# Spreading a load burst, stretching a norm with its shift as a channel bias, and moving operand splits between phases and engines

## The chip, the cores and the metric

The kernel runs on one core of a Trainium2 chip. The metric is the device time of one execution in microseconds (us). The engines are TensorE (PE, with its weight loads listed as PEld), VectorE (DVE), ScalarE (ACT), GpSimd (POOL) and SyncE (SP). Each has its own list of instructions, and they wait for one another through semaphores. In this kernel SP issues every DMA, one after the other.

## The reference

One transformer block on `x[1, 2048, 576]` in float32, with an adaptive layer norm whose shifts, scales and gates come from a conditioning vector `c`.

```python
mod = (silu(c) @ w_mod)                       # six rows of 576: sa, ca, ga, sb, cb, gb
h = layernorm(x) * (1 + ca) + sa
q = (h @ wq), 32 heads of 128                 # k, v from caches of 16 heads, the last 512 positions
o = softmax(q k^T / sqrt(128)) v
x = x + ga * (o @ wo)                         # wo: 4096 x 576
h = layernorm(x) * (1 + cb) + sb              # the second norm
x = x + gb * ((sigmoid(h @ w_gate) * (h @ w_up)) @ w_down)     # F = 4608
```

## The kernel before

Every product is made of three matmuls: an operand is split into a high part in the fp32r format (ACT copies it) and the low rest (a subtraction on DVE or POOL), and hi x hi, hi x lo and lo x hi are added in PSUM. The three large products of the second half are computed by a seven-product scheme on 2 x 2 blocks (as Strassen's), so that sums of weight blocks and of activation blocks are needed besides the blocks themselves. The 2048 rows of `x` are four blocks of 512 (`xs[0]` to `xs[3]`), and a block has four tiles `t` of 128 rows.

The program has three phases.

*Attention*, 0 to about 1420 us. A loop over N = 512 steps, one for each pair of a head and a block, with query projection, scores (`st`, `qt`, `kt`), softmax (`pp`, `ptt`), and the product with v (`ot`). The softmax sums `rs` go out to memory (`rscr<-rs`) and come back as a broadcast (`rb<-rscr`), by which DVE scales the output (`ov`); `oscr<-ov` stores it. Work in the background of the steps is written with `at_n(n, ...)`, which runs a function at step n. A planner lays out a list `jobs` of weight preparations that use parts of `xs` as rooms: `ab` and `tail` jobs make the sums of gate and up weights, split the tail rows and store them in `wsc`; `wo` jobs scale the output weights by the first gate, sum and split them and store them in `wosc`; `down` jobs scale the down weights and store their sums, unsplit, in `dsc`. Every `tail` job ends with small stores `wsc<-x` (24 in all, in four parts). The modulation rows for scale, shift and gates are fetched every 32 steps (`wm`, `wmt`).

*Projection*, about 1420 to 1844 us. VISITS = 32 visits `v`, each of seven stages of 12 matmuls (128x288), of which every stage adds its PSUM result to `x` on DVE. The values come from `vr<-oscr`, are summed on POOL (`vt`, four operations a visit) and split on ACT and DVE (`vh`); the weights come from `wosc` into slots `wb` and `wc`. `late_step` runs in the last steps of attention and issues the first loads of this phase; `beside(v, s)` runs after each stage, and in the last eight visits it takes the statistics of blocks 0 and 1 (`ln_stats`, `ln_ready`), normalizes their tiles (`early_norm(t)`) and makes the sums of the seven-product scheme (`early_sums(t)`), which are put in the scratch tensor `scr[0]`. `park_x` stores the residual rows. `stage_first` reads `scr[0]` back into the tiles `ts` and the rooms in `xs`; `load_combo` transposes a combination by PE (`w<-ident`), and ACT and DVE split it from PSUM into `hc`.

*FFN*, about 1844 us to the end. U = 72 units (36 for each pair of blocks), each of seven products of 7 matmuls (128x512, `a`, `b`, `c`), with the matmuls of the down product of earlier units (`w<-sd,hl`, three of 128x288 at a time) between them. After each product `split_w` splits the next gate/up operand (ACT `sw<-sr`, DVE `sw<-sr,sw`; five buffers) and `load_w` loads a later one (`sr<-wsc`, four buffers). After each four down groups `split_sd` splits a down operand (ACT, POOL `sd<-dr,sd`) and `load_sd` loads one (`dr<-dsc`, three buffers). The gating products (`g`, `v`) are on DVE and ACT, their sums `vs` and splits `hl` on POOL and ACT. At u = 4, 9, 14 and 19 `late_tile` does the second norm of a tile of blocks 2 and 3 and puts its sums in `scr[1]`.

What sets the order: an engine's instructions stand in program order, and `pin` keeps single instructions at the place where they are written against the scheduler, so the hand-written positions decide what stands ahead of what on each queue.

## Time and profile before

| | us |
|---|---|
| median of 3 runs | 3145.04 (3144.78 to 3145.11) |
| the profiled execution | 3147.1 |
| span in its profile | 3145.3 |
| mean granted TensorE clock of the span | 0.986 |
| PE busy | 3048.5 (97%) |
| DVE, ACT, POOL busy | 2288.3, 1721.0, 1655.2 |

The profile is of one execution. PE's busy time is near the span, so the idle time of PE and the stretches in which its granted clock is below 1 are what can be read as lost. A row of the timeline has the start, the duration, the engine, the line of the source (here always that of a helper, so the names of the tiles tell the rows apart), output and inputs, and in brackets the idle time of the engine just before it and what ended that.

### The profile page before, as it was taken

What the parts mean: (1) busy time and instruction counts of PE and PEld (TensorE: products, weight loads), DVE (VectorE), ACT (ScalarE), POOL (GpSimd) and SP (SyncE); (2) the same over time, 40 slices, a digit from 0 to 9 for tenths busy, and PEclk for the clock granted to TensorE, in tenths of its full rate; (3) what the DMA queues carried; (4) which work ended last, traced back from release to release, by engine and by line L of the source; (5) the groups of instructions that cost most, each with busy time, mean ns of one, the idle gap of its engine ahead of it and who ended that gap; (6) DMA issues with size and microseconds to landing.
All of it is one profiled execution on the core that took longest, in us unless ns stands there. A gap on an engine that the chain in (4) does not pass through costs nothing.

```text
span 3145.3 us, 49956 instructions
## 1 busy us (share of the span) xinstructions
PE 3048.5 (97%) x16629; PEld 2619.5 (83%) x16629; DVE 2288.3 (73%) x4116; ACT 1721.0 (55%) x3569; POOL 1655.2 (53%) x1531
## 2 busy tenths in 40 slices
PE   8999999999999999998999889999999989999998
PEld 6888788878888888887999777888888878888887
DVE  6666666687666666666888868777777877777778
ACT  5666555656666655553333344555555645555553
POOL 2344333335666555303555626766665665665664
PEclk9999999999999999999999899999999999999999
DMA  4677877775777766547545254434434443343342
GB/s 118 182 197 213 216 189 191 178 197 137 216 225 219 217 197 195 154 126 269 185 170 185 104 201 144 130 108 131 143 111 115 135 149 112 107 117 111 111 123 79
DMA packets 435570, 503.86 MB, mean 160 GB/s; under 512 B 51184, under 2 KB 392816, under 8 KB 426096
## 3 DMA queue, kind: packets, MB, share of 16 engines
q1 hardware_dynamic: 434704, 500.67, 54.3%
q8 instruction: 131, 2.15, 0.3%
q14 instruction: 127, 1.04, 0.1%
q10 hardware_dynamic: 608, 0.00, 0.0%
HBM read 347.72 MB, written 152.81 MB: 159 GB/s over the span
## 4 chain that ended last, share of the span: by engine, by line
PE 87%; DVE 5%; POOL 3%; DMA 3%; issue 2%; ACT 1%; SPq 1%; ACTq 0%; DVEq 0%; POOLq 0%
PE a L36 19%; PE st L36 18%; PE qp L36 13%; PE w L36 12%; PE ot L36 11%; PE c L36 10%; PE b L36 5%; DVE x L36 2%; POOL x L36 1%; DMA rscr<-rs 1%; DMA sr<-wsc 1%; SPq L36 1%; DVE sw L36 1%; POOL h L36 0%; DVE v L36 0%
## 5 line engine op out<-in xcount | busy, mean ns | idle before, releaser
L36 PEld LDWEIGHTS w<-sd,hl 128*128 128x128 f32 x3036 | 516.5, 189 | 109.7 <-DVE x L36 18.6
L36 PE MATMUL a<-hc,sw 128*128 128x512 f32 x2016 | 588.5, 396 | 15.9 <-DVE v L36 13.9
L36 PE MATMUL w<-sd,hl 128*128 128x288 f32 x3036 | 574.5, 299 | 15.5 <-DVE x L36 14.5
L36 DVE TENSOR_TENSOR x<-w,x 128x288 f32<-128x288 f32 x980 | 429.3, 452 | 197.2 <-PE w L36 192.2
L36 DVE TENSOR_REDUCE neg<-st 128x1 f32<-128x512 f32 x512 | 352.4, 688 | 280.1 <-PE st L36 279.9
L36 ACT ACTIVATE ptt<-st 128x512 fp32r<-128x512 f32 x512 | 306.1, 598 | 433.9 <-PE st L36 433.4
L36 PE MATMUL ot<-ptt,vs 128*128 128x512 f32 x1536 | 486.1, 425 | 1.7 <-DVE ptt L36 1.7
L36 PE MATMUL st<-kt,qt 128*128 128x512 f32 x1536 | 447.0, 398 | 4.0 <-ACT pp L36 4.0
L36 PE MATMUL qp<-hTm,wa 128*128 128x512 f32 x1536 | 446.9, 400 | 3.9 <-DVE qt L36 2.1
L36 DVE TENSOR_TENSOR ptt<-st,ptt 128x512 fp32r<-128x512 f32 x512 | 351.9, 688 | 133.4 <-ACT ptt L36 132.6
L36 PEld LDWEIGHTS a<-hc,sw 128*128 128x128 f32 x2016 | 356.3, 189 | 56.9 <-DVE v L36 17.6
L36 ACT ACTIVATE pp<-st,neg 128x512 f32<-128x512 f32 x512 | 350.3, 684 | 48.2 <-DVE neg L36 47.7
L36 DVE TENSOR_TENSOR sw<-sr,sw 128x256 fp32r<-128x256 f32 x504 | 289.8, 576 | 101.9 <-ACT sw L36 75.1
L36 PEld LDWEIGHTS st<-kt,qt 128*128 128x128 f32 x1536 | 289.2, 189 | 71.6 <-ACT pp L36 5.6
L36 PEld LDWEIGHTS qp<-hTm,wa 128*128 128x128 f32 x1536 | 286.3, 189 | 72.0 <-DVE qt L36 5.5
L36 ACT ACTIVATE sw<-sr 128x384 fp32r<-128x384 f32 x504 | 259.0, 515 | 153.6 <-issue 83.3
L36 POOL TENSOR_TENSOR x<-x 128x256 f32<-128x256 f32 (+3 forms) x334 | 246.7, 758 | 153.6 <-DMA x<-in_B_w_up_dram 101.1
L36 PEld LDWEIGHTS st<-ident,pp 128*128 128x128 f32 x2048 | 255.6, 141 | 77.4 <-issue 4.3
L36 PE MATMUL st<-ident,pp 128*128 128x128 f32 x2048 | 308.8, 274 | 5.3 <-DVE rs L36 2.8
L36 POOL TENSOR_TENSOR sd<-dr,sd 128x288 fp32r<-128x288 f32 x249 | 217.2, 874 | 181.3 <-ACT sd L36 181.3
L36 PE MATMUL c<-hc,sw 128*128 128x512 f32 x1008 | 304.5, 395 | 0.0
L36 PEld LDWEIGHTS ot<-ptt,vs 128*128 128x128 f32 x1536 | 253.6, 191 | 28.1 <-DVE ptt L36 3.1
(168 smaller groups left out, 4747.1 us busy)
## 6 DMA issues: line engine op xcount, KB each, us to landing
sr<-wsc SPq DMA_DIRECT2D x504, 192.0 KB
dr<-dsc SPq DMA_DIRECT2D x249, 144.0 KB
rb<-rscr SPq DMA_DIRECT2D x128, 256.0 KB
oscr<-ov SPq DMA_DIRECT2D x64, 512.0 KB
vr<-oscr SPq DMA_DIRECT2D x32, 1024.0 KB
wsc<-x SPq DMA_DIRECT2D x36, 896.0 KB
wosc<-x SPq DMA_DIRECT2D x32, 1008.0 KB
dsc<-x SPq DMA_DIRECT2D x17, 1008.0 KB
```

What stands on the lines that cost most here:

```text
L36: i = got(*args, **kw)
```

## The change

1. `late_step` issues the five loads `w_load(0, s)` at k = 1, 3, 5, 8 and 11 of the last steps and the second `v_load` at k = 13, where all stood at k = 0. The loop that allocated PSUM tags `w`, `b` and `c` at the start of the projection, with no work in it, is gone; the tags get their banks in the order of use.
2. The second norm of blocks 0 and 1. The shift row is not added to the tiles any more. `shift_cols` (at step 110 of attention) turns the row into columns `fcol` by six PE transposes of one row, and `load_combo` applies it as a bias for each channel: ACT Identity with bias, and one DVE operation with two inputs and a scalar. The scale is multiplied on POOL for block 0 and on DVE for block 1. The steps for a tile stand five stages apart (norm, scale, two puts, sums, four puts), `park_x` goes tile by tile, and the first `stage_first` and `load_combo` stand at other stages.
3. `late_tile` loses its two POOL additions of the shift.
4. The planner has two lists, `jobs` (ab, tail) and `wide` (wo, down), with a due time for each. `down` jobs split their sums (ACT and POOL) and store both parts; `dsc` is twice as large, and in `dsc` and `wosc` the high and low parts are axis 1.
5. In the FFN `load_sd` loads the split operand (`sd<-dsc`, 288 KB, seven buffers); `split_sd` and `dr` are gone. The low part of `split_w` is made on POOL and DVE in turn.
6. The calls between projection and FFN stand in another order.

The core of the diff, without the parts on layout:

```diff
         if k == 0:
             v_load(0)
-            for s in range(5):
-                w_load(0, s)
+        if k in (1, 3, 5, 8, 11):
+            w_load(0, (1, 3, 5, 8, 11).index(k))
+        if k == 13:
             v_load(1)
...
-    for tag, bufs in (("w", 4), ("b", 1), ("c", 1)):
-        for _ in range(bufs):
-            fpsum(tag, bufs, [P, BLK])
...
     def early_norm(t):
+        for b in range(2):
+            h = xs[b][:, t, :]
+            nc.scalar.activation(h, h, AF.Identity, scale=LN[b][1][:, t : t + 1], bias=NMR[b][:, t : t + 1])
+
+    def early_scale(t):
         for b, eng in ((0, nc.gpsimd), (1, nc.vector)):
             h = xs[b][:, t, :]
-            mv, y = LN[b][:2]
-            nc.scalar.activation(h, h, AF.Identity, scale=y[:, t : t + 1], bias=NMR[b][:, t : t + 1])
-            nc.gpsimd.tensor_mul(h, h, rows2["scale"])
-            eng.tensor_add(h, h, rows2["shift"])
+            eng.tensor_mul(h, h, rows2["scale"])
...
-            nc.scalar.activation(hc[:, s, :], p, AF.Copy)
-            if s < 2:
-                nc.vector.tensor_sub(hc[:, 3 + s, :], p, f32(hc[:, s, :]))
+            kind = {B11: 0, T3: 2}.get(c, 1)
+            if c in (T1, T4):
+                nc.scalar.activation(hc[:, s, :], p, AF.Copy)
             else:
-                r = slice(P // 2, P)
-                nc.vector.tensor_sub(hc[r, 2, :], p[r], f32(hc[r, 2, :]))
+                nc.scalar.activation(hc[:, s, :], p, AF.Identity, bias=fcol[:, kind, s : s + 1])
+            r, to = (slice(0, P), 3 + s) if s < 2 else (slice(P // 2, P), 2)
+            if c in (T1, T4):
+                nc.vector.tensor_sub(hc[r, to, :], p[r], f32(hc[r, s, :]))
+            else:
+                nc.vector.scalar_tensor_tensor(hc[r, to, :], p[r], fcol[r, kind, s : s + 1], f32(hc[r, s, :]),
+                                               op0=OP.add, op1=OP.subtract)
...
+    def shift_cols():
+        row = rows2["shift"]
+        p = ps_wo()
+        for half in range(2):
+            e = wp.tile([P, 4, TQ], F32, tag="hd", name="hd", bufs=1)
+            n0 = half * D2
+            pin(nc.gpsimd.tensor_copy(e, row[:, None, n0 + 2 * P : n0 + D2].to_broadcast([P, 4, TQ])))
+            for k in range(3):
+                src = row[0:1, n0 + k * P : n0 + (k + 1) * P] if k < 2 else e.rearrange("p q d -> p (q d)")[0:1]
+                pin(nc.tensor.transpose(p[:, 3 * half + k : 3 * half + k + 1], src, ident[0:1, 0:1]))
...
+    at_n(110, shift_cols)
...
-        nc.vector.tensor_sub(t[:, 3:5], r[:, 0:2], f32(t[:, 0:2]))
+        turn[0] += 1
+        (nc.gpsimd if turn[0] % 2 else nc.vector).tensor_sub(t[:, 3:5], r[:, 0:2], f32(t[:, 0:2]))
...
-            t = fpool["p"].tile([P, D2], F32, tag="dr", name="dr", bufs=3)
-            d = nc.sync.dma_start(t, dsc[g % NG][:, a if g == GL else WITH[a]])
+            t = fpool["p"].tile([P, 2, D2], F32R, tag="sd", name="sd", bufs=7)
+            d = nc.sync.dma_start(f32(t), dsc[g % NG][:, :, a if g == GL else WITH[a]])
...
-            nc.gpsimd.tensor_add(h, h, rows2["shift"])
...
     for _ in range(4):
         load_w(True)
+    for k in range(4, 10):
+        stage_first(k)
     for _ in range(4):
         split_w()
-        load_w(True)
-    for k in range(4, 10):
-        stage_first(k)
     load_combo(0, 1, True)
     for k in range(10, 14):
         stage_first(k)
-    for _ in range(3):
-        load_sd(True)
-    for _ in range(5):
-        split_sd()
+    for _ in range(4):
+        load_w(True)
+    for _ in range(7):
         load_sd(True)
```

How the rows of the queues move, at three places. On SP, where attention ends and the projection's first loads are issued, before:

```order
L36 DMA vr<-oscr_0_286 128x2048
L36 DMA wb_15152<-wosc_354 128x2304
L36 DMA wb_15154<-wosc_354 128x2304
L36 DMA wb_15156<-wosc_354 128x2304
L36 DMA wb_15158<-wosc_354 128x2304
L36 DMA wb_15160<-wosc_354 128x2304
L36 DMA vr<-oscr_0_286 128x2048
L36 DMA rscr_284<-rs 128x4
L36 DMA rb<-rscr_284 128x512
L36 DMA rscr_285<-rs 128x4
L36 DMA rb<-rscr_285 128x512
L36 DMA oscr_3_293<-ov 512x1x256 x2
```

and now:

```order
L36 DMA vr<-oscr_0_286 128x2048
L36 DMA rscr_284<-rs 128x4
L36 DMA wb_15276<-wosc_354 128x8x288
L36 DMA rb<-rscr_284 128x512
L36 DMA wb_15318<-wosc_354 128x8x288
L36 DMA rscr_285<-rs 128x4
L36 DMA wb_15353<-wosc_354 128x8x288
L36 DMA rb<-rscr_285 128x512
L36 DMA oscr_3_293<-ov 512x1x256
L36 DMA wb_15380<-wosc_354 128x8x288
L36 DMA wb_15395<-wosc_354 128x8x288
L36 DMA oscr_3_293<-ov 512x1x256
```

The five weight loads stood ahead of the last two trips of the softmax sums; now they stand among them, the second `vr` behind all of them. Of the fetch of the last modulation row on SP, near step 114: 18 tail stores (`wsc_312`, `wsc_313`, `wsc_314`, six each) stood in the rows just ahead of it, and six stand there now.

On POOL, at the last four visits of the projection (`x_101` is block 0, `x_102` block 1, the digits behind `scale` and `shift` are buffer numbers), before:

```order
L36 TENSOR_TENSOR vt<-vr,vt 128x512
L36 TENSOR_TENSOR x_101<-x_101,scale_2152 128x576
L36 TENSOR_TENSOR x_101<-x_101,shift_3131 128x576
L36 TENSOR_TENSOR x_101<-x_101,scale_2152 128x576
L36 TENSOR_TENSOR x_101<-x_101,shift_3131 128x576
L36 TENSOR_TENSOR x_101<-x_101,scale_2152 128x576
L36 TENSOR_TENSOR x_101<-x_101,shift_3131 128x576
L36 TENSOR_TENSOR vt<-vr 128x512
L36 TENSOR_TENSOR x_101<-x_101,scale_2152 128x576
L36 TENSOR_TENSOR x_102<-x_102,scale_2152 128x576
L36 TENSOR_TENSOR vr<-vr 128x4x128
L36 TENSOR_TENSOR x_101<-x_101,shift_3131 128x576
```

and now:

```order
L36 TENSOR_TENSOR vt<-vr,vt 128x512
L36 TENSOR_TENSOR x_101<-x_101,scale_2153 128x576 x3
L36 TENSOR_TENSOR vt<-vr 128x512
L36 TENSOR_TENSOR vr<-vr 128x4x128
L36 TENSOR_TENSOR x_101<-x_102,x_101 128x288
L36 TENSOR_TENSOR vt<-vt,vr 128x512
L36 TENSOR_TENSOR x_101<-x_101,scale_2153 128x576
L36 TENSOR_TENSOR x_102<-x_102,x_101 128x288
L36 TENSOR_TENSOR vt<-vr,vt 128x512
L36 TENSOR_TENSOR x_101<-x_102,x_101 128x288
L36 TENSOR_TENSOR x_102<-x_102,x_101 128x288
L36 TENSOR_TENSOR vt<-vr 128x512
```

The run of multiplications and additions is gone; three multiplications of block 0 stand together in the queue, and the sums of the scheme (`x_101<-x_102,x_101`) come among the `vt` sums. In the source those three are five stages apart; they are not pinned, so the order of the built program has them where their inputs are ready.

On SP, where the FFN's first loads are issued (`scr_294` is `scr[0]`), before:

```order
L36 DMA scr_294<-x_101 128x288
L36 DMA scr_294<-x_102 128x288 x2
L36 DMA scr_294<-x_101 128x288
L36 DMA ts<-scr_294 128x576 x4
L36 DMA sr<-wsc_300 128x384 x6
L36 DMA sr<-wsc_301 128x384
L36 DMA sr<-wsc_300 128x384
L36 DMA x_101<-scr_294 128x576 x4
L36 DMA x_102<-scr_294 128x576 x4
L36 DMA ts<-scr_294 128x576 x2
L36 DMA dr<-dsc_336 128x288 x3
```

and now:

```order
L36 DMA scr_294<-x_102 128x288
L36 DMA ts<-scr_294 128x576 x4
L36 DMA scr_294<-x_101 128x288
L36 DMA scr_294<-x_102 128x288 x2
L36 DMA scr_294<-x_101 128x288
L36 DMA sr<-wsc_300 128x384 x4
L36 DMA x_101<-scr_294 128x576 x4
L36 DMA x_102<-scr_294 128x576 x4
L36 DMA ts<-scr_294 128x576 x2
L36 DMA sr<-wsc_300 128x384 x2
L36 DMA sr<-wsc_301 128x384
```

Four `sr` loads stand ahead of the reads of `scr[0]` where eight stood, and the `ts` reads stand ahead of the last tile's puts.

More of the change, by code (lines that the diff above doesn't have):

```diff
@@ L686, in adaln_block_kernel @@
             jobs.append(("tail", f - 3))
-    jobs += [("wo", g) for g in range(H // 2)] + [("down", g) for g in range(NF // 2)]
+    wide = [("wo", g) for g in range(H // 2)] + [("down", g) for g in range(NF // 2)]
     BG = {}
@@ L761, in bg_split @@
     def bg_split(k, part):
-        if jobs[k][0] == "tail":
+        if k[0] == "tail":
             r, m, hi = BG[k]
@@ L765, in bg_split @@
         else:
-            a, b = ((0, 4), (4, 7))[part]
+            a, b = ((0, 4), (4, 8 if k == ("down", NF // 2 - 1) else 7))[part]
             v, hi = BG[k][0][:, a:b], BG[k][1]
@@ L782, in bg_store @@
                 pin(nc.sync.dma_start(wsc[f][:, :, 0:2], BG[k][:, 0:7]))
-            elif kind == "down":
-                n = 8 if f == NF // 2 - 1 else 7
-                pin(nc.sync.dma_start(dsc[f][:, :n], BG[k][0][:, :n]))
-            else:
-                for i in range(2):
-                    pin(nc.sync.dma_start(wosc[f // 4][:, :, i, f % 4], BG[k][1 - i][:, :7]))
-    free = {0: 9, 1: 9, 2: 7, 3: 7}
-    n = 9
-    for k, (kind, f) in enumerate(jobs):
-        need = 2 if kind == "wo" else 1
-        while True:
-            got = sorted((free[r], r) for r in range(NB) if free[r] <= n and
-                         n < N - 46 and not (r > 1 and n1 - 50 < n < n1 + 4))
-            if len(got) >= need:
-                break
+                return
+            n = 8 if k == ("down", NF // 2 - 1) else 7
+            for i in range(2):
+                to = wosc[f // 4][:, i, f % 4] if kind == "wo" else dsc[f][:, i, :n]
+                pin(nc.sync.dma_start(to, BG[k][1 - i][:, :n]))
+    free = {0: 9, 1: 9, 2: 7, 3: 7}
+    n, due = 9, 9.0
+    while jobs or wide:
+        assert n < N - 44, (n, len(jobs), len(wide))
+        got = [r for _, r in sorted((free[r], r) for r in range(NB) if free[r] <= n)
+               if not (r > 1 and n1 - 50 < n < n1 + 4)]
+        two = n > 130 and len(got) > 1 and wide and (not jobs or not n1 - 50 < n < n1 + 4)
+        if due > n or not got or not (two or jobs):
             n += 1
-            assert n < N
-        rooms = [r for _, r in got[:need]]
+            continue
+        k = (wide if two else jobs).pop(0)
+        kind = k[0]
+        rooms = got[: 2 if two else 1]
         for r in rooms:
-            free[r] = n + 14
+            free[r] = n + {"ab": 10, "tail": 13}.get(kind, 12)
         at_n(n, bg_load, k, rooms)
```

102 lines of the change are left out of this document (52 added, 50 removed).

## The prediction

> **What bounds the kernel now.** I read the head of the page first: the engine shares.
>
> ```profile
> span 3145.3 us, 49956 instructions
> PE 3048.5 (97%) x16629; PEld 2619.5 (83%) x16629; DVE 2288.3 (73%) x4116; ACT 1721.0 (55%) x3569; POOL 1655.2 (53%) x1531
> ```
>
> TensorE is busy for 97% of the span. The change removes almost no matmul work, so it can only win time in which PE idles or runs at a low granted clock. The second view is therefore a table by stage (window; busy us and instructions of PE, PEld, DVE, ACT, POOL; granted clock; DMA share; GB/s).
>
> ```profile
> ...
> 360.00:380.00 20.00, 16.40 (x72) 13.16 (x71) 9.73 (x16) 11.93 (x28) 9.12 (x12) 0.83 0.90 247
> ...
> 750.00:1300.00 550.00, 550.00 (x2827) 451.66 (x2826) 373.12 (x580) 353.59 (x754) 339.24 (x301) 1.00 0.70 208
> 1430.00:1460.00 30.00, 16.43 (x96) 14.62 (x95) 11.36 (x18) 5.78 (x12) 5.28 (x5) 0.77 0.77 269
> 1500.00:1750.00 250.00, 250.00 (x1877) 250.00 (x1876) 216.83 (x325) 98.91 (x156) 141.00 (x91) 1.00 0.47 174
> 1770.00:1850.00 80.00, 57.02 (x343) 53.55 (x343) 57.36 (x101) 26.48 (x44) 40.43 (x34) 0.83 0.34 114
> 1850.00:1960.00 110.00, 97.61 (x487) 81.52 (x488) 83.31 (x182) 57.05 (x117) 60.33 (x60) 0.95 0.57 186
> 1960.00:2240.00 280.00, 273.22 (x1449) 237.28 (x1448) 204.62 (x420) 147.98 (x304) 196.32 (x170) 0.99 0.44 130
> 2300.00:2350.00 50.00, 50.00 (x270) 43.74 (x269) 36.52 (x76) 27.22 (x56) 28.91 (x26) 1.00 0.40 113
> 2520.00:2560.00 40.00, 30.83 (x150) 25.71 (x149) 31.23 (x56) 15.88 (x34) 30.45 (x29) 0.91 0.56 176
> ...
> ```
>
> What a stage loses is its length less busy time times clock. That gives 6.4 at 360-380, 17.3 at 1430-1460, 32.7 at 1770-1850, 17.3 at 1850-1960, 9.5 at 1960-2240 and 11.9 at the pair turnover (2520-2560): 95 us, which is what the change works on. The stretches 750-1300, 1500-1750 and 2300-2350 lose nothing: PE is full at clock 1.00. The start of the kernel, the norm of blocks 2 and 3 and the kernel's last matmuls lose time too, but the change does not touch them.
>
> **The change, part by part.**
>
> *Modulation weights (360-380).* ACT waits for their fetch, and PE for ACT.
>
> ```profile
> 352.00 7.20 SPq L36 DMA_DIRECT2D wsc<-x  x10
> 361.35 0.97 SPq L36 DMA_DIRECT2D wm<-in_w_mod_dram  x2
> 366.09 1.82 ACT L36 ACTIVATE wm<-wm,cexp 128x288 f32<-128x288 f32 x4 [3.62 <-DMA wm<-in_w_mod_dram]
> 372.71 1.65 PE L36 MATMUL st<-kt,qt 128*128 128x512 f32 x3 [3.60 <-ACT pp L36]
> ```
>
> Ten tail stores take SP 7.20 us, 0.72 each. In the order of before 18 tail stores stand close ahead of this fetch; in the new order 6 do. Twelve fewer are 8.6 us, more than the 3.62 that ACT waits. Gain 5 of the 6.4, between 2 (another transfer ends last) and 6.4.
>
> *Planner and shift columns.* The down operands are now split in the attention: 18 jobs of two ACT copies and two POOL subtractions, and twice the stores. The nearest work is that of the wo jobs in 750-1300: there POOL is busy 339 of 550 us, ACT 354, DMA 0.70, and PE 550.00. With as much room left I cost it at nothing; the cover is ACT's and POOL's idle third there. Without it, the next thing late would be ACT's `pp`, as in the row at 372.71. The shift columns need six one-row PE transposes and two POOL copies (`hd`) that stand behind the weight sums. POOL waits for the loads of these sums in the row of `x<-x`:
>
> ```profile
> L36 POOL TENSOR_TENSOR x<-x 128x256 f32<-128x256 f32 (+3 forms) x334 | 246.7, 758 | 153.6 <-DMA x<-in_B_w_up_dram 101.1
> ```
>
> If PE meets one such wait it loses some us, otherwise under 1 us. I take a loss of 1, between 0 and 6.
>
> *Start of the projection (1430-1460).* SP issues two `vr` and five `wb` loads (128x2048 and 128x2304 words, 1.05 and 1.18 MB each, 8.0 MB) ahead of the last two softmax-sum round trips.
>
> ```profile
> 1417.72 4.46 SPq L36 DMA_DIRECT2D wb<-wosc  x5
> 1424.70 0.32 SPq L36 DMA_DIRECT2D rscr<-rs  x1
> 1441.81 0.32 SPq L36 DMA_DIRECT2D rb<-rscr  x1
> 1449.28 1.05 DVE L36 TENSOR_TENSOR ov<-ot,rb 128x512 f32<-128x512 f32 x1 [3.17 <-DMA rb<-rscr]
> 1450.38 3.25 PE L36 MATMUL a<-wb,vh 128*128 128x288 f32 x12 [12.85 <-DVE ov L36]
> 1459.92 1.76 PE L36 MATMUL b<-wc,vh 128*128 128x288 f32 x12
> ```
>
> The store of the sums goes out at 1424.70 and SP is let go at 1441.81, 17.1 us later; PE stands 12.85 us for the DVE `ov` that needs the result. In the new order one `wb` stands ahead of the first of these round trips and two more ahead of the second's broadcast, and the first `a` matmul waits for no DVE result any more: its PSUM bank is an attention score bank. So most of the 12.85 goes. What is late next is weights: with a load every second or third step the last `wb` and the first `wc` go out later than now. 8.0 MB between 1417.72 and 1441.81 are 332 GB/s at the least; 9.2 MB up to the first `wc` take 28 us at that rate, so 1445 if SP never waited, against 1459.92 for the first `wc` stage now. SP will wait some steps for `rs`, so I take 1451, gain 9, between 5 (those waits spread the loads further) and 13 (the whole stall goes).
>
> *End of the projection (1770-1850).* POOL runs eight multiplications and four additions of the second norm (1.55 for the one shown), among the `vt` sums; SP waits with the puts of the results, and with it the `vr` load behind them.
>
> ```profile
> 1774.44 0.15 DVE L36 TENSOR_TENSOR ln_a<-ln_y 128x4 f32<-128x4 f32 x1
> 1776.64 1.55 POOL L36 TENSOR_TENSOR x<-x,scale 128x576 f32<-128x576 f32 x1 [4.21 <-ACT x L36]
> 1776.81 1.40 DVE L36 SCALAR_TENSOR_TENSOR ln_y<-ln_a,ln_y 128x4 f32<-128x4 f32 x1
> 1779.72 25.50 SPq L36 DMA_DIRECT2D scr<-x  x6
> L36 DVE TENSOR_TENSOR vh<-vr,vh 128x512 fp32r<-128x512 f32 x109 | 109.8, 1008 | 6.4 <-ACT vh L36 4.8
> L36 DVE TENSOR_TENSOR vh<-vt,vh 128x512 fp32r<-128x512 f32 x81 | 76.4, 944 | 17.0 <-ACT vh L36 17.0
> L36 DVE TENSOR_TENSOR x<-a,x 128x288 f32<-128x288 f32 x109 | 49.1, 450 | 10.2 <-PE a L36 10.1
> L36 DVE TENSOR_TENSOR x<-x,shift 128x576 f32<-128x576 f32 x4 | 4.9, 1224 | 2.7 <-POOL x L36 2.7
> L36 DVE TENSOR_TENSOR x<-x 128x288 f32<-128x288 f32 x4 | 3.9, 986 | 4.8 <-POOL x L36 4.8
> 1841.31 1.84 PE L36 MATMUL a<-wc,vh 128*128 128x288 f32 x12
> ```
>
> (The groups `vh` and `x<-a` are of 1460-1765, the two other groups of 1770-1845; the rest are single rows.) After the change POOL has four such multiplications instead of twelve operations (three of them still together on its queue), and the puts of a tile come two to six stages behind its norm, so a `vr` load meets shorter waits ahead of it. The chain POOL-SP-`vr` dissolves, and DVE is late next. Its work from 1768 on: about 24 small norm operations at 0.37 mean between the 0.15 and 1.40 shown, 8.8; 25 `vh` at 0.99 (mean of the rows), 24.7; 26 `x` at 0.45, 11.7; four scale multiplications at 1.22, 4.9; eight half-width subtractions at 0.86 (between 0.74 alone and 0.986), 6.9. Sum 57.0, so it ends at 1825; PE's own 22 stages of 12 matmuls, at the 1877 matmuls in 250 us of its full stretch 1.6 us each, are 35 and lie beneath. The last stage ended at 1843.15 before. Gain 18. With `vh` at its undisturbed 0.68 it would be 25; if SP still holds `vr` behind puts that wait for POOL, 8.
>
> The two DVE rows, 0.15 alone and 1.40 while a POOL multiplication of 1.55 runs, are what a rule of the Trainium skill describes (SBUF — State Buffer, "SBUF: two separate sides"): VectorE with two SBUF inputs and GpSimd take the shared port pair as an exclusive lock for a whole instruction. The trace agrees for these rows. By that rule each of DVE's 25 `vh` could wait a whole POOL operation, which would add 25 x 0.3 and end this part near 1832, a gain of 11; the steady rows of 0.94 to 1.01 already hold such waits, so I leave the sum.
>
> *FFN start (1850-1960) and late tiles.*
>
> ```profile
> 1848.54 4.47 SPq L36 DMA_DIRECT2D x<-scr  x8
> 1853.56 2.20 PE L36 MATMUL w<-ident,x 128*128 128x128 f32 x8 [5.15 <-DMA x<-scr]
> 1931.20 1.62 POOL L36 TENSOR_TENSOR h<-h,shift 128x576 f32<-128x576 f32 x1
> 1932.84 4.25 SPq L36 DMA_DIRECT2D scr<-h  x2
> 1948.62 1.09 PE L36 MATMUL w<-sd,hl 128*128 128x288 f32 x3 [2.81 <-DVE x L36]
> ```
>
> PE loses 5.15 us, and some at a lower clock, to `x<-scr` loads that SP issues after eight weight loads; the new order has four ahead of them (at the 0.56 us an issue that 4.47 for eight gives, 2.2 us of SP sooner, and 0.8 MB less in flight), and the puts they read come out spread. The first late tile loses about 6 because SP stands at `scr<-h` while POOL works through multiplications, shift additions, `hl` and `sd`; two of its additions (1.6 us each) and the `sd` subtractions go. Of 17.3 lost I take 12, between 0 and 16: nothing if POOL's new `sw` work takes the place of `sd`. The three other late tiles lose 9.5 by the same chain; gain 5, between 0 and 8. The pair turnover keeps its DVE and DMA work; gain 1, between 6 and a loss of 6.
>
> *Splits in the FFN.* The steady FFN loses nothing, so nothing is won there. What moves:
>
> ```profile
> L36 POOL TENSOR_TENSOR sd<-dr,sd 128x288 fp32r<-128x288 f32 x249 | 217.2, 874 | 181.3 <-ACT sd L36 181.3
> L36 DVE TENSOR_TENSOR sw<-sr,sw 128x256 fp32r<-128x256 f32 x504 | 289.8, 576 | 101.9 <-ACT sw L36 75.1 <-PE w L36 23.5
> ```
>
> POOL gives up 217 us of `sd` and takes 252 `sw` subtractions, 191 us at the 0.758 of its 128x256 row; DVE gives up 145, ACT its `sd` copies. `sd` loads double: 249 x 144 KB more, 36 MB over 1290 us, 28 GB/s on 113 at a DMA share of 0.40. All lighter or with room; the cover is the lead of four products with which a split runs ahead (a product with its downs is some 12.75 matmuls, 2.37 us at 270 in 50 us, so 9.5 us). A queue that is in order can still make a product late, so I allow a loss of 2, between 0 and the rival's 50 below.
>
> Sum: -5 +1 -9 -18 -12 -5 -1 +2 = -47. Against the profiled execution's own 3147.1 that is 3100.1; the median of the runs is 3145.04, 2.1 less, so 3098.
>
> **Rivals.**
> 1. *DVE and the puts still bound the projection's end, and the FFN start keeps its waits.* For it: DVE is at 217 of 250 us even in steady state. Against: 25.50 us of SP waiting go with POOL's chain. Terms at 8, 5 and 4 instead of 18, 9 and 12: 3098 + 22 = 3120.
> 2. *POOL's `sw` makes products late: the slower end.* POOL's `vs` and `hl` come in runs of 1.3 to 1.5 us each and wait for ACT and DVE; a `sw` in the queue behind them can miss its product. Price: 72 units x delay. It decides from 47 / 72 = 0.65 us a unit; at 0.75 the time is 3098 + 54 = 3152. Against: the 9.5 us of lead, and POOL 29 of 50 busy. The Trainium skill warns here (GPSIMD Engine Reference, "Performance versus the Vector engine"): GpSimd takes about twice VectorE's time for two-input elementwise work. By its ratio a moved `sw` takes 1.15, 3.5 of them a unit 1.4 us more than the trace's price, and were that all exposed it would cost 100 us. The trace has 0.758 against 0.576, ratio 1.3, and measurement decides.
> 3. *More comes: late tiles and turnover stalls go as well.* Terms at 25, 13, 16, 8 and 4 give 3098 - 21 = 3077.
> 4. *The start wait is not removed, since scheduling keeps PE behind `rb`.* Then 9 is lost: 3107, inside the forecast's own range.
>
> **How the numbers follow.** The measurement of this kernel tells apart about 0.2%, 6.3 us. My forecast (3086 to 3110) has 0.50; rival 1 (to 3126) 0.25; rival 3 0.15; rival 2 0.10, of which 0.06 ends above 3151, 0.02 within 0.2% and the rest is faster. So faster 0.92, same 0.02, slower 0.06. The range 3075 to 3127 leaves out rival 2 and part of rival 3's and rival 1's ends.
>
> **What would show it.** Right: in 360-380 the 3.62 and 3.60 us waits are gone; no 12.85 before the first `a<-wb`; the last `a<-wc` ends near 20 us closer to the end of attention; POOL has no run of x multiplications and SP no 25 us at `scr<-x`; the FFN windows still read PE 50.00 with some 270 matmuls, DVE near 31 and POOL near 28 us. Wrong: fewer than 266 matmuls in 50 us of steady FFN with PE waiting for POOL `sw` or DVE; a PE wait for POOL `hd` near 345 us; a PE wait for `wc` at the projection's start as long as the old one.

## The result, and the profile after

The changed kernel takes 3107.07 us (median of 4 runs, 3105.21 to 3109.53) against 3145.07: a ratio of 0.9877 with a 95% interval of 0.986 to 0.9894, 38 us faster. The forecast was 3098 with a range of 3075 to 3127. The profiled execution took 3107.64, its span is 3105.9.

```profile
span 3105.9 us, 49158 instructions
PE 3028.0 (97%) x16635; PEld 2602.8 (84%) x16635; DVE 2184.5 (70%) x3866; ACT 1680.7 (54%) x3356; POOL 1682.8 (54%) x1556
```

The table by stage of the changed kernel, with the columns of the table of before:

```profile
360.00:380.00 20.00, 19.95 (x105) 16.32 (x104) 12.52 (x20) 15.30 (x35) 11.44 (x15) 1.00 0.79 197
660.00:700.00 40.00, 28.25 (x132) 22.46 (x131) 35.90 (x74) 14.28 (x34) 20.03 (x20) 0.87 0.60 169
1430.00:1460.00 30.00, 23.46 (x125) 19.50 (x123) 17.26 (x28) 10.28 (x23) 5.48 (x4) 0.89 0.91 292
1770.00:1850.00 80.00, 66.04 (x438) 62.48 (x437) 66.18 (x117) 34.12 (x56) 36.70 (x37) 0.94 0.56 180
1850.00:1960.00 110.00, 101.02 (x516) 84.52 (x515) 77.67 (x174) 55.98 (x108) 66.69 (x65) 0.98 0.56 177
1960.00:2240.00 280.00, 278.09 (x1500) 242.67 (x1500) 187.67 (x378) 135.56 (x255) 182.56 (x167) 1.00 0.56 166
2300.00:2350.00 50.00, 50.00 (x271) 43.73 (x271) 32.56 (x67) 23.68 (x45) 27.03 (x25) 1.00 0.53 153
```

PE is full at 360-380 now. The end of the projection (1770-1850) loses 80 - 66.04 x 0.94 = 17.9 where it lost 32.7, and the late tiles (1960-2240) 1.9 where they lost 9.5. But 660-700, where the prediction expected no change, loses 40 - 28.25 x 0.87 = 15.4. In the kernel before it lost 40 - 36.17 x 0.91 = 7.1:

```profile
660.00:700.00 40.00, 36.17 (x170) 28.59 (x169) 38.66 (x88) 18.79 (x42) 21.12 (x20) 0.91 0.65 185
```

Fixed windows shift against the work when the work moves. So I followed one DVE instruction of each step, visit or unit through both timelines and took the difference of its start times; a step of this running difference is what a place gained or lost. Its last value, -40.3, is the whole difference of the two profiled executions but for the last microsecond, so nearly all of it has a place.

```
changed kernel less kernel before, at the same instruction, us
attention (neg<-st):   step 32 +0.3 | 64 +2.7 | 112 +3.1 | 128 -0.7 | 224 -1.7 | 240 +5.5 | 288 +5.2 | 304 +7.2 | 496 +5.8 | 511 +6.5
projection (x<-b):     visit 1 +6.2 | 24 +6.2 | 27 +6.2 | 28 +3.9 | 29 -4.9 | 31 -7.6
FFN (g<-a):            unit 0 -16.2 | 2 -8.4 | 6 -14.9 | 24 -24.9 | 36 -26.5 | 40 -33.8 | 66 -38.0 | 71 -40.3
```

Between units 0 and 2 the changed kernel loses 7.8 us of its gain again, and 6.5 come back by unit 6. PE waits 4.5 us there, for ACT and POOL, where it waited 1.7 before. Every kernel of the experiments loses 5.8 us or more at this place, so none of the edits explains it, and its cause is open.

Three waits of the changed kernel answer to three of before. The chain of the modulation fetch is gone. The start of the projection and the norm of blocks 2 and 3 have waits of their own (PE rows):

```profile
688.94 1.09 PE L36 MATMUL st<-ident,pp 128*128 128x128 f32 x4 [9.77 <-DVE rs L36]
...
1449.97 2.35 PE L36 MATMUL a<-wb,vh 128*128 128x288 f32 x12 [2.50 <-DVE x L36]
1454.16 3.22 PE L36 MATMUL c<-wb,vh 128*128 128x288 f32 x12 [1.84 <-DMA wb<-wosc]
```

The row of before that answers to the first; the two others take the place of the 12.85 before the first `a<-wb`:

```profile
681.21 0.63 PE L36 MATMUL st<-ident,pp 128*128 128x128 f32 x4 [2.85 <-DVE rs L36]
```

### The profile page after: what moved, and what is told of

Its sections match the earlier page's. It is cut to its first block, busy times and chain, and to the rows that moved or that the text cites. A ratio compares the mean times of both kernels' runs of the same rounds, so it can differ in the third digit from the quotient of the medians.

```text
span 3105.9 us, 49158 instructions
## 1 busy us (share of the span) xinstructions
PE 3028.0 (97%) x16635; PEld 2602.8 (84%) x16635; DVE 2184.5 (70%) x3866; ACT 1680.7 (54%) x3356; POOL 1682.8 (54%) x1556
## 4 chain that ended last, share of the span: by engine, by line
PE 86%; DVE 5%; DMA 3%; POOL 2%; issue 1%; ACT 1%; SPq 1%; ACTq 0%; DVEq 0%; POOLq 0%
PE a L36 19%; PE st L36 17%; PE qp L36 12%; PE w L36 12%; PE ot L36 10%; PE c L36 10%; PE b L36 5%; DVE x L36 1%; SPq L36 1%; POOL x L36 1%; POOL hl L36 1%; DMA sr<-wsc 1%; DMA raw<-in_A_wq_dram 0%; POOL vs L36 0%; DVE vh L36 0%
## 5 line engine op out<-in xcount | busy, mean ns | idle before, releaser
L36 DVE TENSOR_TENSOR x<-w,x 128x288 f32<-128x288 f32 x980 | 436.4, 453 | 295.6 <-PE w L36 291.8
L36 PE MATMUL w<-sd,hl 128*128 128x288 f32 x3036 | 563.8, 295 | 6.6 <-DVE x L36 3.7
L36 POOL TENSOR_TENSOR sw<-sr,sw 128x256 fp32r<-128x256 f32 x252 | 205.3, 816 | 307.0 <-ACT sw L36 212.3
L36 PE MATMUL st<-ident,pp 128*128 128x128 f32 x2048 | 308.5, 273 | 13.8 <-DVE rs L36 10.8
L36 POOL TENSOR_TENSOR wa<-raw,wa 128x512 fp32r<-128x512 f32 (+1 forms) x128 | 112.2, 876 | 255.8 <-ACT wa L36 221.9
```

What stands on the lines that cost most here:

```text
L36: i = got(*args, **kw)
```

## The experiments

Each kernel below is the changed kernel with one edit. What is compared is the running difference to the kernel before, place by place, since single executions differ by some microseconds in places that an edit does not touch. How much can be read from the kernels whose edit lies elsewhere: their gain is -0.4 to 1.3 us over the start of the projection (last attention step to second visit), 21.9 to 24.8 from visit 24 to unit 0, 30.4 to 35.1 from visit 24 to unit 24, and 6.9 to 7.6 at the turnover (units 36 to 40). A difference inside such a span shows nothing.

**Start of the projection.** The spread, and the PSUM banks, taken back one at a time, and loads between the two.

`e1_burst`:

```diff
         if k == 0:
             v_load(0)
-        if k in (1, 3, 5, 8, 11):
-            w_load(0, (1, 3, 5, 8, 11).index(k))
-        if k == 13:
+            for s in range(5):
+                w_load(0, s)
             v_load(1)
```

> The changed kernel with its spread undone: all five w_load(0, s) and the second v_load stand at k = 0 again, while the PSUM loop stays out. Theory A (the spread only trades one wait for another: with the bank wait on ov gone, the loads should go out early): the first a stage starts near 1440 and the first b stage of the projection, which is 6.7 us later than before in the changed kernel and 6.5 us later already at the end of attention, gains 6 to 9 us; the whole 3098 to 3101. Theory B (the spread is what shortens the start, because the last rb comes sooner): PE stands for rb as before, 6 us lost against the changed kernel, 3113.

`e8_mid` has `w_load(0, k)` at k = 0 to 4 and `v_load(1)` at k = 5.

> The changed kernel with the loads between: w_load at k = 0 to 4, second v_load at k = 5. Theory A (late arrival of the weights bounds the start): the gain lies between the changed kernel and the burst or beyond the burst, 4 to 8 us, 3099 to 3103. Theory B (rb bounds): as the changed kernel, 3107, or some us worse.

`e2_banks` puts the loop `for tag, bufs in (("w", 4), ("b", 1), ("c", 1))` back.

> The changed kernel with the loop that allocates the PSUM tags w, b and c put back, so the first a matmul waits for DVE's last ov again. Theory A (start bound by the arrival of weights, the bank wait hidden beneath it): the first a starts 3 to 5 us later, but the eighth visit within 1 us of the changed kernel; 3107. Theory B (the bank wait was half of the stall): 5 us lost through to the end; 3112.

Between the last attention step and the second visit the changed kernel goes from +6.5 to +6.2 (gain 0.3), the burst from +6.0 to +8.4 (loss 2.4), the loads between from +8.4 to +7.9 (gain 0.5), and the kernel with the banks put back from +3.4 to +3.6 (loss 0.2). The whole times are 3107.4 (3106.59 to 3108.22), 3105.5 (3103.26 to 3107.32) and 3106.01 (3100.97 to 3111.71). Only the burst lies outside the scatter, so the spread is worth some 2 to 4 us, and the loads between and the banks make no difference that can be told. For the banks that is theory A. With them back, the first `a` waits for DVE's `ov` again, and by the second visit nothing of it is left:

```profile
1446.72 3.25 PE L36 MATMUL a<-wb,vh 128*128 128x288 f32 x12 [5.53 <-DVE ov L36]
```

For the loads between, the gain of 4 to 8 us of theory A did not come. Neither theory on the burst holds: the `a` matmuls start early in it, and then PE waits for DVE all the same. SP and PE of the burst:

```profile
1422.48 13.28 SPq L36 DMA_DIRECT2D wb<-wosc  x5
...
1443.61 1.75 PE L36 MATMUL a<-wb,vh 128*128 128x288 f32 x12
1445.20 1.76 PE L36 MATMUL c<-wb,vh 128*128 128x288 f32 x12
1458.29 3.25 PE L36 MATMUL a<-wb,vh 128*128 128x288 f32 x12 [11.33 <-DVE x L36]
```

PE runs two stages and stands 11.33 us at the third, whose bank is free only when DVE has added the first result to `x`; that addition stands on DVE behind the `ov` that waits for `rb`. The wait moved by two stages. And the first row shows what neither theory had: five loads take SP 13.28 us to issue where they took 4.46 before. The change had laid `wosc` out as [P, 2, 4, 7, D2], so a load of one product picks eight runs of 288 words (1152 B) in each partition where it read one run of 9216 B.

`e10_layout`:

```diff
-    wosc = [dram.tile([P, 2, 4, 7, D2], ...
+    wosc = [dram.tile([P, 7, 2, 4, D2], ...
-                to = wosc[f // 4][:, i, f % 4] if ...
+                to = wosc[f // 4][:, :, i, f % 4] if ...
-        pin(nc.sync.dma_start(f32(WHL[q, s]), wosc[q][:, :, :, STAGES[s][1]]))
+        pin(nc.sync.dma_start(f32(WHL[q, s]), wosc[q][:, STAGES[s][1]]))
```

> The changed kernel with wosc laid out as before, [P, 7, 2, 4, D2], so that a weight load of the projection reads one run of 9216 B in each partition where the changed kernel reads eight of 1152 B (its stores are cut into seven runs of 1152 B instead). Theory A (the cut loads cost the start its gain: five wb loads took SP 13.28 us against 4.46 before, and 355 GB/s against 413): wb issues fall from 0.53 to about 0.4 us, the rate rises to about 400 GB/s, and between the end of attention and the second visit the kernel gains 3 to 8 us on the kernel before, where the changed kernel gains 0.3; 3100 to 3104. Theory B (DVE's x additions behind the last ov bound the start, whatever the loads): within 1.5 us of the changed kernel there; 3107.

3101.95 us (3101.6 to 3104.21). The start goes from +6.1 to +3.7, a gain of 2.4 on the kernel before and of 2.1 on the changed one. `e12_best` below has this layout too and gains 2.7 there; both lie outside the scatter. Issue rows of the same loads, of the changed kernel and of this one:

```profile
1430.81 0.58 SPq L36 DMA_DIRECT2D wb<-wosc  x1
...
1445.08 2.14 SPq L36 DMA_DIRECT2D wb<-wosc  x2
```

```profile
1430.61 0.38 SPq L36 DMA_DIRECT2D wb<-wosc  x1
...
1444.14 1.74 SPq L36 DMA_DIRECT2D wb<-wosc  x2
1449.52 2.08 PE L36 MATMUL a<-wb,vh 128*128 128x288 f32 x12 [2.45 <-DVE x L36]
1452.86 3.22 PE L36 MATMUL c<-wb,vh 128*128 128x288 f32 x12 [1.26 <-DMA wb<-wosc]
```

The cut loads are part of the lost gain, less than theory A said; the DVE wait and later weights stay. The rate of all transfers in 40 equal slices, of the kernel before from 1417 to 1442 us and of the burst from 1417 to 1460:

```profile
GB/s 0 20 36 72 102 125 321 439 419 421 452 428 413 442 428 413 457 428 398 457 398 457 413 413 442 428 428 457 383 442 469 367 401 406 421 407 199 27 13 0
```

```profile
GB/s 347 118 8 2 0 0 57 112 394 396 371 389 375 353 360 357 356 355 356 357 358 353 359 356 361 385 442 389 100 8 10 170 66 0 38 202 350 142 0 274
```

The same weights came at 398 to 457 GB/s before and at 353 to 361 in most slices of the burst.

**Norm of blocks 2 and 3.** On DVE of the changed kernel twelve operations on four columns (a reciprocal square root by Newton steps) follow one another in 10.1 us. The first four take 1.31 to 1.42 us each, and each ends 0.02 to 0.03 us behind the end of a POOL operation; the other eight take 0.16 to 1.18. DVE and POOL rows of the changed kernel:

```profile
677.13 1.42 DVE L36 TENSOR_SCALAR ln_v<-mv 128x4 f32<-128x4 f32 x1
678.58 1.33 DVE L36 TENSOR_SCALAR ln_y<-ln_v 128x4 int32<-128x4 int32 x1
679.95 1.32 DVE L36 TENSOR_SCALAR ln_y<-ln_y 128x4 int32<-128x4 int32 x1
...
676.73 3.15 POOL L36 TENSOR_TENSOR h<-h,scale 128x576 f32<-128x576 f32 x2 [4.51 <-DVE h L36]
679.85 2.74 POOL L36 TENSOR_TENSOR h<-h,shift 128x576 f32<-128x576 f32 x2
```

`e7_norm3` has `norm_block(3, n1 - 28, ...)` instead of `norm_block(3, n1 - 24, ...)`.

> The changed kernel with the statistics of block 3 four steps earlier, so that DVE's twelve small Newton operations of block 3 (1.3 us each in a row in the changed kernel, where POOL runs h multiplications and additions at that time, against 0.16) stand before POOL's multiplications begin. Theory A (a DVE operation with its operands in SBUF waits for a whole POOL operation): the chain takes 0.16 to 0.2 us an operation, the 9.77 us wait of PE for rs at 689 goes or shrinks under 3 us, and the 7.2 us that this place loses become 0 to 2; 3100 to 3102. Theory B (the place loses because DVE is full there, in any order): the loss stays within 2 us of 7.2; 3107.

```profile
674.05 0.12 DVE L36 TENSOR_SCALAR ln_y<-ln_v 128x4 int32<-128x4 int32 x1
674.17 0.17 DVE L36 TENSOR_SCALAR ln_v<-mv 128x4 f32<-128x4 f32 x1
674.25 0.16 DVE L36 TENSOR_SCALAR ln_y<-ln_y 128x4 int32<-128x4 int32 x1
...
681.56 1.09 PE L36 MATMUL st<-ident,pp 128*128 128x128 f32 x4 [6.70 <-DVE rs L36]
711.10 0.99 PE L36 MATMUL qp<-hTm,wa 128*128 128x512 f32 x3 [4.07 <-DVE qt L36]
```

3106.73 us (3104.26 to 3108.26). The operations take 0.12 to 0.17 us with POOL idle, so it is shown that POOL's operations held them. The time is not saved: steps 224 to 240 lose 1.3 instead of 7.2 us, though PE still stands 6.70 once, behind statistics and `h` operations that DVE now has in a bunch; but 5.2 more go by step 288, 4.07 of it at 711 behind an `ov` that waits 4.46 us for its `rb`. By step 288 the place has lost 6.5 against 6.9. Theory A holds for the operations. For the time the number of theory B came out, but its reason is not shown: DVE was busier here before the change, 38.66 of 40 us against 35.90, when the window lost less than half as much.

**End of the projection.** `e6_scale_dve` has `((0, nc.vector), (1, nc.vector))` in `early_scale`, so POOL does none of the scale multiplications.

> The changed kernel with the scale multiplications of block 0 on DVE too: POOL loses four operations of 1.4 to 1.9 us at the projection's end, DVE takes four more. Theory A (whole-instruction blocking between POOL and DVE: the three multiplications in a row cost DVE the 1.03, 1.35 and 1.32 us at 1783 to 1787): the end of the projection is 0 to 4 us earlier in spite of 3 us more DVE work; 3103 to 3107. Theory B (DVE is the bound and every operation added to it counts): 3 to 6 us later; 3110 to 3113.

3103.86 us (3101.93 to 3104.22). From visit 24 to visit 28 this kernel gains 4.7 us on the kernel before, where the changed one gains 2.3 and no kernel with its edit elsewhere more. By unit 0 it is 24.8 against 22.4, and 24.8 lies at the end of the scatter, so what is left of the 2.4 can't be told. Theory B is refuted: with four more operations on DVE nothing comes later. This kernel's Newton chain stays at 0.15 to 0.16 us an operation between 1777 and 1785.8, where POOL is idle; in the changed kernel three in a row take 1.03 to 1.35 beside POOL's multiplications.

```profile
1783.54 1.03 DVE L36 SCALAR_TENSOR_TENSOR ln_a<-ln_a,ln_v 128x4 f32<-128x4 f32 x1
1784.61 1.35 DVE L36 SCALAR_TENSOR_TENSOR ln_y<-ln_a,ln_y 128x4 f32<-128x4 f32 x1
1785.99 1.32 DVE L36 TENSOR_TENSOR ln_a<-ln_y 128x4 f32<-128x4 f32 x1
...
1783.10 4.19 POOL L36 TENSOR_TENSOR x<-x,scale 128x576 f32<-128x576 f32 x3 [4.72 <-ACT x L36]
```

**FFN start.** `e5_ffn_order`:

```diff
     for _ in range(4):
         load_w(True)
-    for k in range(4, 10):
-        stage_first(k)
     for _ in range(4):
         split_w()
+        load_w(True)
+    for k in range(4, 10):
+        stage_first(k)
     load_combo(0, 1, True)
     for k in range(10, 14):
         stage_first(k)
-    for _ in range(4):
-        load_w(True)
```

> The changed kernel with the order of calls at the FFN start undone: four split_w with four more loads of sr ahead of the reads of scr, as before. Theory A (the eight sr loads ahead of x<-scr made the 5.15 us wait): 3 to 6 us back between the last projection stage and the second unit; 3110 to 3113. Theory B (the late puts of the last norm tile made it): within 1 us of the changed kernel.

```profile
1827.82 15.35 SPq L36 DMA_DIRECT2D sr<-wsc  x8
1843.22 4.47 SPq L36 DMA_DIRECT2D x<-scr  x8
1848.24 2.21 PE L36 MATMUL w<-ident,x 128*128 128x128 f32 x8 [4.74 <-DMA x<-scr]
```

3111.91 us (3110.14 to 3117.38). From visit 24 to unit 0 it gains 17.3 instead of 22.4: 5.1 us come back, as theory A said and outside the scatter, with the wait that the kernel before had (5.15). By unit 24 3.2 of the 5.1 are left.

**Late tiles.** `e4_late_adds` puts two POOL additions back in `late_tile`, of the scale row where the shift was, so the values of blocks 2 and 3 are other ones.

> The changed kernel with two POOL additions put back in each late tile (the scale row is added where the shift was, so the values of blocks 2 and 3 are not the reference's). Theory A (the chain of POOL operations in a late tile, with SP waiting behind its puts, is what stalls): 1 to 2.5 us back for each of four late tiles, 3111 to 3117. Theory B (the room comes from the down splits that left POOL): under 1 us in all.

3124.8 us (3121.8 to 3129.1). From visit 24 to unit 24 it gains 16.5 instead of 31.1: eight additions, 12.8 us of POOL at 1.6 each, cost 14.6 us of the end. That is more than theory A allowed (4 to 10 in all), and theory B is refuted. PE at one late tile of this kernel, and of the changed one:

```profile
2109.57 0.73 PE L36 MATMUL a<-hc,sw 128*128 128x512 f32 x2 [2.98 <-POOL sw L36]
2115.71 1.65 PE L36 MATMUL a<-hc,sw 128*128 128x512 f32 x3 [3.70 <-DVE v L36]
```

```profile
2100.88 0.74 PE L36 MATMUL a<-hc,sw 128*128 128x512 f32 x2 [1.86 <-POOL sw L36]
```

**Splits of the gate and up weights.** `e3_sw_dve` and `e9_sw_pool` replace `(nc.gpsimd if turn[0] % 2 else nc.vector)` by the one engine or the other.

> The changed kernel with all 504 low parts of split_w on DVE, as before. Theory A (relief of DVE by the sharing carries the FFN's gain beyond what was predicted: turnover, steady drift): of the 8 us that the turnover gained at least 4 come back, and of the 0.1% by which a unit of the steady FFN is shorter most; 3115 to 3120. Theory B (what counts is that POOL and ACT lost the down splits; DVE has room): 3104 to 3109, and late tiles better by 1 to 3 us, as POOL has still less to do.

> The changed kernel with all 504 low parts of split_w on POOL, the prediction's second rival driven to its end: POOL takes 206 us more, DVE 145 less. Theory A (the lead of four products covers a split on either engine; all on DVE cost nothing): the steady FFN still reads PE full, but late tiles and turnover, where POOL is full, lose 4 us each: 3115 to 3130. Theory B (rival 2: POOL's queue makes products late in every unit): PE waits for POOL sw in the steady FFN, 0.3 us or more a unit, 3130 or more.

All on DVE: 3106.36 us (3105.07 to 3108.45). All on POOL: 3106.08 (3103.47 to 3106.36). Half and half: 3107.07. The steady windows of the two:

```profile
2300.00:2350.00 50.00, 50.00 (x271) 43.77 (x271) 35.57 (x78) 24.00 (x45) 18.67 (x14) 1.00 0.52 142
```

```profile
2300.00:2350.00 50.00, 50.00 (x272) 43.76 (x271) 28.11 (x58) 23.53 (x45) 33.83 (x35) 1.00 0.56 156
```

PE is full in both, with DVE at 35.57 and 28.11 and POOL at 18.67 and 33.83 of 50 us. From visit 24 to the end they gain 46.0 and 46.7 us, the changed kernel 46.5. The sharing of these splits is worth nothing in the whole time, and it costs nothing. So the time of theory A on all-DVE fails, and so do the times of both theories on all-POOL; theory B on all-DVE has the time, but the late tiles are no better for it (10.2 us from unit 6 to 24 against 10.0). At the turnover the sharing does show: units 36 to 40 take 71.8 us with all of them on DVE, 72.6 half and half and 74.5 with all on POOL (79.8 before the change), and the first and the last lie outside the scatter.

**POOL work for the down operands.** `e11_pool_sd` puts a subtraction on POOL for every down operand.

```diff
             if t == TPB - 1:
+                w = SD[g, a]
+                dm = fpool["p"].tile([P, D2], F32, tag="dm", name="dm", bufs=1)
+                nc.gpsimd.tensor_sub(dm, f32(w[:, 0]), f32(w[:, 1]))
                 load_sd()
```

> The changed kernel with a POOL subtraction of 128x288 put back for every down operand (into a tile that nobody reads; ACT's half of the split stays out), so POOL has about the 217 us of work that left it, besides the sw parts. Theory A (POOL's queue made the pair turnover and the late tiles slow, and its relief is where the unpredicted gain of the FFN came from): 5 to 8 us back at the turnover and 3 to 8 at the late tiles; 3115 to 3125. Theory B (the relief was ACT's, or the splits' place in the chain of a down product): within 3 us of the changed kernel. The 0.1% of the steady unit comes back under neither, or else it was POOL's.

3431.44 us (3429.13 to 3435.09), outside both theories. It is no test of POOL's load: the subtraction stands on POOL soon after the load of the operand it reads, which nothing else needs so early, and POOL waits for that transfer. POOL rows, and the waits of 2300 to 2400:

```profile
2308.16 0.73 POOL L36 TENSOR_TENSOR sw<-sr,sw 128x256 fp32r<-128x256 f32 x1
2313.22 0.81 POOL L36 TENSOR_TENSOR dm<-sd 128x288 f32<-128x288 f32 x1 [4.34 <-DMA sd<-dsc]
```

```profile
POOL dm L36 <- DMA sd<-dsc: 42.1, 15, 4.3
ACT sw L36 <- DMA sr<-wsc: 37.1, 22, 3.2
```

POOL is busy 29.07 of 50 us there, no more than in the kernel before. But the `sw` parts behind each wait come late; SP's next `sr` load waits for the buffer that such a `sw` frees (in these 100 us SP waits 70.7 us for POOL `sw`), and the `sd` load behind that on SP is the one POOL waits for next. The three close a loop, and this kernel is 324 us slower than the changed one.

**What the runs point to.** `e12_best` is the changed kernel with the layout of `e10_layout`, the scale multiplications of `e6_scale_dve`, those of `late_tile` on DVE as well, and `mod_sum` at n + 4 instead of n + 3.

> The changed kernel with what the other runs point to: the scale multiplications of blocks 0 and 1 on DVE (3.6 us earlier at the end there), wosc laid out as before (3.5 us), the sums of the modulation rows one step later (mod_sum at n + 4, for the 2.4 us that the fetch at step 50 costs), and the scale multiplications of the late tiles on DVE too (POOL loses eight more operations). Theory A (a POOL operation in a late tile costs some 2 us of the end, as the eight additions put back cost 16; whatever is left of the late tiles' 6 us goes): 3107 - 3.6 - 3.5 - 2 - 4 = 3094, 3090 to 3098. Theory B (the late tiles are now bound by DMA round trips and not by POOL, and places do not add): 3098 to 3102.

3098.15 us (5 runs, 3093.74 to 3102.0), ratio to before 0.9852 with an interval of 0.9837 to 0.9866. The median is 9 us below the changed kernel's. Each against the kernel before as it was measured beside it, the gains are 45.7 and 38.0 us, and the two intervals overlap from 0.986 to 0.9866, so the whole times alone do not settle it. By place: steps 32 to 64 lose 0.3 instead of 2.4, visits 24 to unit 0 gain 26.1 instead of 22.4, and to unit 24 39.2 instead of 31.1, all outside the scatter. In the FFN's first 400 us the two PE waits for POOL `sw` (2.53 and 1.86) are gone, and units 6 to 24 gain 11.9 instead of 10.0, so theory A holds there; the median came out 4 above its sum, at the edge of theory B's span.

## Why the prediction was right, and where its terms were wrong

The forecast of 47 us was 9 too many, inside the range, and nearly every term was off. That it came so near is in good part luck: the attention lost 9.9 us or so, and the turnover and the steady units gained some 15, where the prediction had put next to nothing.

| place | predicted | measured (running difference) |
|---|---|---|
| modulation fetch | -5 | -3.8 (steps 112 to 128) |
| shift columns | +1 | +0.4 (64 to 112) |
| rest of attention | 0 | +2.4, +7.2 and +2.0 at steps 32-64, 224-240 and 288-304; about -1.7 elsewhere |
| projection start | -9 | -0.3 |
| projection end | -18 | -13.8 (visits 24 to 31) |
| FFN start with the first late tile | -12 | -7.3 (visit 31 to unit 6) |
| late tiles | -5 | -10.0 (units 6 to 24) |
| turnover | -1 | -7.3 (units 36 to 40) |
| steady units, end, new waits | +2 | -1.6, -4.2, -2.3 (units 24-36, 40-66, 66-71) |

*Modulation fetch*: right, by the mechanism given. The waits of 3.62 and 3.60 us are gone. The same fetch 64 steps earlier became 2.4 us slower, which the prediction did not consider; a step more between fetch and use takes 2.1 of it away (`e12_best`). The PE wait for POOL `hd`, named as a sign of being wrong, came with 1.01 us at 349, well inside its term.

*Projection start*: the failed step is "most of the 12.85 goes". It went from the first `a` and came back behind it. "What is late next is weights" was one part of three. Behind the wait stood DVE's first `x` addition behind the same `ov` (11.33 us in the burst, 2.50 with the spread), the arrival of weights, and loads cut into runs an eighth as long, whose price the prediction set at nothing by taking the rate of before. The layout is a line of the diff that the prediction did not cost; it is worth some 2 us.

*Projection end*: the mechanism held, at 13.8 of 18. SP still stands long at `scr<-x`, but the last `vr` load now goes out behind 7.10 us of it where it stood behind 25.50, and DVE was late next, as said: PE waits 10.2 us for `x` additions and `vh`, and 1.9 for a norm operation.

```profile
1784.58 7.10 SPq L36 DMA_DIRECT2D scr<-x  x2
1791.77 0.38 SPq L36 DMA_DIRECT2D vr<-oscr  x1
1806.69 0.46 DVE L36 TENSOR_TENSOR x<-x 128x288 f32<-128x288 f32 x1 [1.43 <-POOL x L36]
```

The size of DVE's work was right: the terms of the sum (57.0) measure 9.7 for 27 small norm operations at 0.36, 21.9 for 25 `vh` at 0.88, 12.5, 5.0 and 7.2, together 56.3. What failed is that the sum let DVE work without a pause: from 1774.2 us (the 1768 of before) to the end of its last addition it is 62.3 us, and in 8 to 9 of them DVE stood idle, in 5.1 for POOL's part of the half-width subtractions. No run puts the shift additions or the old places of the steps back, so how the 13.8 divide among them is open. The Trainium skill's rule (SBUF — State Buffer, "SBUF: two separate sides") is borne out by the hold: 0.16 us against 1.3 for the same operation. The 11 that the prediction got from it came near the 13.8 by luck, since it stood on `vh` of 1.29 and they took 0.88.

*660-700*: "the change does not touch them" was wrong. The norm's own code is the same, so the planner's new jobs, which share its engines, are the likeliest to have moved it; no run takes them back. In the kernel before, block 3's chain met POOL's operations as well (two of 1.38 and 1.40 us), but PE waited only 2.85 us for it, against 9.77. Why the place loses some 7 us in either order (`e7_norm3`) is open.

*FFN start and late tiles*: 12 and 5 were predicted, 7.3 and 10.0 measured; that the sums agree (17 and 17.3) is luck. The `x<-scr` wait fell to the new order, 5.1 us (`e5_ffn_order`). Under-sized was a POOL addition in a late tile: 14.6 us for eight (`e4_late_adds`), more than their busy time. That the `sw` parts wait behind them is shown by the 2.98 us of PE; what SP's puts add is argued.

*Turnover and steady units*: 7.3 and some 6 us that the prediction did not have. The sharing is not their cause (`e3_sw_dve` has them too). At the turnover PE's waits fall from 9.2 to 4.5 us; the longest of before, and of now:

```profile
2554.77 1.65 PE L36 MATMUL a<-hc,sw 128*128 128x512 f32 x3 [4.76 <-DVE v L36]
```

```profile
2520.03 0.73 PE L36 MATMUL a<-hc,sw 128*128 128x512 f32 x2 [1.83 <-POOL sw L36]
```

In the kernel before, that `v` stood on DVE behind an addition that waited for `x<-xscr`, which SP issued late; in the 56 us up to there SP waited 10.2 us for POOL `sd`, more than for anything else. This, and the 71.8 to 74.5 us above, make it likely that the down splits' leaving POOL gave the turnover's gain. But SP now waits as long for POOL's `x` and `sw` (12.1 and 9.6 us in 55), and `e11_pool_sd`, meant to show it, measured something else, so it stays argued.

For the steady units the failed step is "the steady FFN loses nothing, so nothing is won there". PE is full at clock 1.00 in both kernels, and yet a unit takes 16.85 us where it took 17.01 (units 42 to 66), 0.9% less. From one `w<-sd,hl` matmul to the next it is 0.132 us instead of 0.135, and within the `a` products 0.231 instead of 0.233. Of the experiments all but `e11_pool_sd` have the 16.85, so no edit that was tried makes the difference; why is open.

*Rival 2* is right in mechanism and wrong in place and price: PE does wait for POOL `sw`, 2.53 and 1.86 us at two late tiles and 1.83 at the turnover, and not in steady units, so 0.65 us a unit was never near. The first of these rows:

```profile
1930.09 0.73 PE L36 MATMUL a<-hc,sw 128*128 128x512 f32 x2 [2.53 <-POOL sw L36]
```

GpSimd's price was 0.816 us a `sw` against 0.758 predicted, 1.4 times DVE's 0.576 and not twice, as the Trainium skill's rule would have it (GPSIMD Engine Reference, "Performance versus the Vector engine"). All of them on either engine gave the same whole time, which fits the lead of four products.

## What to carry to other kernels

A wait that is taken away shows the next one: follow what frees the buffer two stages on, not only the first instruction that waits. Before a transfer is moved, read in the diff how long its contiguous runs are; an axis moved in a scratch tensor can take back what the new schedule gives. Work moved to a half-idle engine was free here while everything in that queue had its inputs; one operation there that waits for a late transfer stops all that stands behind it, whatever the busy share says. A sum of an engine's work gives its end only if the engine never waits, so look for what it shares with others. And an engine that reads full can still have something to win: count the work done in a window too.

## What the runs showed of the hardware

- A GpSimd operation can hold up a VectorE operation on SBUF operands until it ends. A DVE operation on 128x4 words takes 0.12 to 0.17 us with POOL idle and up to 1.42 beside POOL operations of 1.3 to 1.8, and then ends 0.02 to 0.03 us behind one of them. This also holds for operations with one input (`ln_v<-mv`), while `x<-a,x`, with one of its two inputs from PSUM, keeps its 0.44 to 0.46 us beside POOL. The Trainium skill has both halves: single-source operations with source and destination in SBUF can run in a two-port mode (VectorE: DVE Perf Modes, "What auto-detection actually checks"), and such a mode takes the shared ports (SBUF — State Buffer, "SBUF: two separate sides"); the trace agrees as far as the hold goes, and which mode ran no run shows.
- Loads in runs of 1152 B instead of 9216 B: in most slices 353 to 361 GB/s against 398 to 457, and 0.53 to 0.58 us of SP for an issue that meets no wait against 0.36 to 0.44; a burst of five held SP for 13.28 us against 4.46.
- PE can be full at a granted clock of 1.00 and still do 0.9% more in the same time: a steady unit of the same 91 matmuls took 17.01 us before and 16.85 after.
